# Sink rows of v: four small loads and one placement for the whole batch, instead of a selection matmul per sequence

## The chip, the cores and the metric

The kernel runs on one core of one Trainium2 chip. Of its engines five names occur here: PE (TensorE, matrix products; PEld is its weight load), DVE (VectorE), ACT (ScalarE), POOL (GpSimd) and SP (SyncE, which here only issues DMAs and waits). PE and DVE can work on PSUM, where matrix products land; PSUM has eight banks. The metric is the device time of one execution in microseconds (us), lower is better; it is the median of several runs. A profiled execution has a time of its own, and a span (first to last instruction) that is a little shorter than that time.

## The reference

Inputs: q, k, v of shape (batch 4, heads 8, positions 768, head size 64) in float32, two mixing vectors, and three weight matrices. First an attention in which every position sees the last 128 positions and, besides, the first four positions of its sequence (the sinks):

```python
is_sink = pos[None, :] < int(n_sink)          # n_sink = 4
rel = pos[:, None] - pos[None, :]
in_window = (rel >= 0) & (rel < int(window))  # window = 128
scores = np.where(is_sink | in_window, scale * q @ k.T, -1e9)
a = softmax(scores);  x = a @ v               # heads side by side: (4, 768, 512)
```

Its output x goes through a channel mix:

```python
xk = mu_k * x + (1 - mu_k) * x_prev           # x_prev: one position earlier
xr = mu_r * x + (1 - mu_r) * x_prev
k = np.maximum(xk @ w_k, 0)                   # 512 -> 1024  ("keys")
out = sigmoid(xr @ w_r) * (k * k @ w_v)       # "gates", and 1024 -> 512 ("product")
```

## The kernel before

**Units.** The work is cut into 12 units of 256 positions, three per sequence (`b` is the sequence, `T` the unit in it). A unit goes through `prepare` (its rows of q and k are cast to bf16 and transposed, its rows of v are cast into `vb`), `attend` (scores, exponentials `e` on ACT, a mask multiplied in by DVE, products with `vb`, division into `x`), `mix` (`x` transposed into `xt`, then `xk` and `xr` made by DVE) and `ffn` (the keys, `rl` and its square `kk`; the gates and `th`; the product and `ob`, which is stored). The `ffn` of a unit stands in the program beside the attention of the next one.

**The sinks.** The units with T = 1 and 2 also need the four sink positions of their sequence. Their scores come from `ksink`, a copy of four columns of the transposed keys; the exponentials are `es`. For the products with v there is one tile `vsink` of 128 partitions per sequence. Its partitions hold, in blocks of 32 for a pair of heads and of 4 rows for each of the two heads in it, the four sink rows of v for that head, next to a column of ones, and zeros for every other head. It is made like this: a product on PE (L814) with the 0/1 matrix `spread`, which copies rows 0 to 3 of the cast `vb` of the sequence's first unit, with all 512 columns of all heads, to every block; and a multiplication on DVE (L818) of the 512 columns in PSUM with the 0/1 tile `hmask`, which leaves to each partition its own head. This happens once per sequence, so four times, and there are two `vsink` tiles, whose column of ones is written once at the start by POOL (L642).

**PSUM.** Two tiles of two banks each hold scores; the other four banks form one pool ("bank"), from which every other product takes its place: transposes, sink scores, the product of L814, the products with v, keys, gates and products. A bank comes free when the engine that reads it is done.

**What sets the order.** Each operation is entered in a list with `P.op` and has a number. The tables `ORDER` (the sequence of numbers on each engine) and `CHOICE` (which of the engines allowed to an operation does it) are written out in the file; `schedule` (L195) follows them, and picks buffers and banks as it goes. On each engine the instructions run strictly in that sequence, and an instruction that waits holds up all behind it on its engine. Until about 28 us of planned time `schedule` also puts products without use into PE's gaps ("fill", on the tile `warm`).

**The start.** DVE clears tiles (L578 to L588). POOL makes the masks, `hmask`, the identity and `spread` (L594 to L642). ACT issues the two small loads of the mixing vectors, loads its table and runs one tiny exponential (L551, L560). SP issues all loads of q, k, v and the weights, first q and k of unit 0 in two halves each.

## Time and profile before

| what | value |
|---|---|
| median of 3 runs | 163.79 us (162.93 to 163.96) |
| the profiled execution: its time | 163.9 us |
| the profiled execution: its span | 162.2 us, granted PE clock 1.000 |
| busy in the span: PE, DVE, ACT, POOL | 152.7, 147.4, 119.9, 39.3 us |
| moved by DMA | 35.16 MB, mean 217 GB/s |

Busy time of PE counts products without use too, and the ends of products are modelled. The span is 1.7 us shorter than the execution's own time. In the views, a row of a timeline or of the chain begins with its start and its length in us; a row of a group gives busy time in us, the mean length of one instruction in ns, and the idle time of its engine just before the group's instructions, with what ended most of it; a row of waits gives the total in us, how often, and the longest.

### The profile page before, as it was taken

Reading aid. Unit: us, or ns where it says so; the run is one execution under the profiler, and the core shown is the slowest. Engines: PE = TensorE matmul, PEld = TensorE weight load, DVE = VectorE, ACT = ScalarE, POOL = GpSimd, SP = SyncE. Lnnn points to the kernel's source line nnn. Section 1 sums busy time; section 2 is a strip of 40 time slices with the busy share of each in tenths; the row PEclk is TensorE's granted clock in tenths of the full one; section 3 lists DMA queues with packets and bytes.
Section 4 is the critical chain, followed back from the end, with each engine's and each line's share of the span. In section 5 each row is a group of like instructions: output and inputs, shape, how many; then the busy total and the mean of one; then the engine's idle time right before and its main releaser. Section 6 shows DMA issues by size and latency. Waiting matters only on the chain.

```text
span 162.2 us, 4697 instructions
## 1 busy us (share of the span) xinstructions
PE 152.7 (94%) x1857; PEld 99.4 (61%) x1857; DVE 147.4 (91%) x378; ACT 119.9 (74%) x194; POOL 39.3 (24%) x69
## 2 busy tenths in 40 slices
PE   7959779999999999999999999999999999999992
PEld 2545457964568567776566575865466865577541
DVE  6299989999999999999999999999999999998631
ACT  4699998999999899888689964878167985043420
POOL 6643330610662260242111006241010040001000
PEclk9999999999999999999999999999999999999999
DMA  4999999999988999999999999999999733351113
GB/s 140 251 353 249 391 342 295 368 401 312 211 265 215 259 233 156 237 266 144 223 213 211 303 220 207 196 265 164 265 168 206 168 89 103 65 195 68 65 65 129
DMA packets 78885, 35.16 MB, mean 217 GB/s; under 512 B 68744, under 2 KB 71056, under 8 KB 78864
## 3 DMA queue, kind: packets, MB, share of 16 engines
q1 hardware_dynamic: 78384, 33.63, 88.7%
q0 software_dynamic: 320, 1.05, 1.8%
q8 instruction: 14, 0.23, 0.7%
q10 hardware_dynamic: 160, 0.20, 0.3%
q14 instruction: 7, 0.06, 0.1%
HBM read 24.12 MB, written 6.29 MB: 188 GB/s over the span
## 4 chain that ended last, share of the span: by engine, by line
PE 75%; DVE 7%; SPq 5%; DMA 5%; ACT 3%; issue 2%; POOL 1%; DVEq 0%
PE bank L1188 24%; PE bank L1139 22%; PE bank L1170 12%; PE bank L971 6%; DMA ks<-in_k_dram 5%; PE sc L866 5%; SPq L483 2%; DVE e L952 2%; SPq L500 2%; ACT rl L1149 2%; PE bank L1012 2%; PE bank L754 1%; PE bank L924 1%; SPq L507 1%; DVE x L988 1%
## 5 line engine op out<-in xcount | busy, mean ns | idle before, releaser
L1139 PE MATMUL bank<-xk,wk_sb 128*128 128x256 bf16 x384 | 48.3, 273 | 0.0
L938 ACT ACTIVATE e<-sc 128x1024 bf16<-128x1024 f32 (+1 forms) x48 | 45.0, 965 | 2.3 <-PE sc L866 2.1
L1188 PE MATMUL bank<-wv_h,kk 128*128 128x512 bf16 x184 | 44.8, 379 | 0.0
L1139 PEld LDWEIGHTS <-wk_sb 128*128 128x128 bf16 x384 | 36.0, 98 | 7.2
L1149 ACT ACTIVATE rl<-bank 128x512 bf16<-128x512 f32 x47 | 27.2, 608 | 15.6 <-PE bank L1139 13.8
L952 DVE TENSOR_TENSOR e<-e,mask 128x1024 bf16<-128x1024 bf16 (+1 forms) x48 | 31.0, 659 | 0.0
L1188 PEld LDWEIGHTS <-kk 128*128 128x128 bf16 x184 | 17.0, 98 | 15.8
L1061 DVE SCALAR_TENSOR_TENSOR xr<-td,mu_all,xt 128x256 bf16<-128x256 bf16 x48 | 24.0, 514 | 0.0
L1170 PE MATMUL bank<-wr_sb,xr 128*128 128x512 bf16 x96 | 23.7, 379 | 0.4 <-DVE vsink L818 0.4
L1061 DVE SCALAR_TENSOR_TENSOR xk<-td,mu_all,xt 128x256 bf16<-128x256 bf16 x48 | 23.9, 526 | 0.1
L1161 DVE TENSOR_TENSOR kk<-rl 128x512 bf16<-128x512 bf16 x48 | 20.9, 451 | 1.8 <-ACT rl L1149 1.7
L1176 ACT ACTIVATE th<-bank 128x512 f32<-128x512 f32 x24 | 14.1, 598 | 10.9 <-PE bank L1170 10.9
L988 DVE TENSOR_TENSOR x<-bank,rec 128x256 bf16<-128x256 f32 x48 | 19.4, 416 | 0.3
L1197 DVE SCALAR_TENSOR_TENSOR ob<-th,bank 128x512 f32<-128x512 f32 x23 | 15.5, 679 | 2.7 <-ACT th L1176 2.5
L971 PE MATMUL bank<-vb,e 128*128 128x65 bf16 x352 | 16.4, 194 | 1.3 <-DVE e L952 1.2
L791 POOL CAST vb<-vs 128x512 bf16<-128x512 f32 x10 | 9.4, 948 | 31.8 <-DMA vs<-in_v_dram 22.1
L971 PEld LDWEIGHTS <-e 128*128 128x128 bf16 x352 | 13.8, 97 | 5.4 <-DVE e L952 2.5
L1170 PEld LDWEIGHTS <-xr 128*128 128x128 bf16 x96 | 8.8, 98 | 9.3 <-issue 0.5
L866 PEld LDWEIGHTS <-kt 64*64 64x64 bf16 (+1 forms) x496 | 8.9, 106 | 6.4 <-issue 3.8
L866 PE MATMUL sc<-qt,kt 64*64 64x128 bf16 (+4 forms) x496 | 12.6, 226 | 0.0
L1048 DVE TENSOR_TENSOR td<-xt 128x512 bf16<-128x512 bf16 x24 | 10.6, 455 | 0.0
L714 POOL CAST qb<-qs 128x512 bf16<-128x512 f32 x7 | 5.1, 722 | 21.8 <-DMA qs<-in_q_dram 21.8
(95 smaller groups left out, 150.9 us busy)
## 6 DMA issues: line engine op xcount, KB each, us to landing
vs<-in_v_dram SPq DMA_DIRECT2D x24, 256.0 KB, 5.0
out_dram<-ob SPq DMA_DIRECT2D x19, 256.0 KB, 3.9
ks<-in_k_dram SPq DMA_DIRECT2D x16, 256.0 KB, 5.1
qs<-in_q_dram SPq DMA_DIRECT2D x12, 256.0 KB, 4.0
qs<-in_q_dram SPq DMA_DIRECT2D x6, 512.0 KB, 5.8
ks<-in_k_dram SPq DMA_DIRECT2D x4, 512.0 KB, 8.4
w<-in_moe_w_k_dram SPq DMA_DIRECT2D x2, 1024.0 KB, 8.8
w<-in_moe_w_v_dram SPq DMA_DIRECT2D x2, 1024.0 KB, 10.4
```

Of the source, the lines that this page charges most:

```text
L866: nc.tensor.matmul(out=sc[keys, a, o0 + f0 - q0:o0 + f1 - q0], lhsT=lhs[rows, keys], rhs=qs[rows, f0:f1], start=u not in BIAS, stop=True, ...
L938: nc.scalar.activation(out=buf[ek][:, :, lo:], in_=buf[sck][:, :, lo:], func=AF.Exp, scale=scale)
L952: nc.vector.tensor_tensor(out=at, in0=at, in1=m, op=ALU.mult)
L971: nc.tensor.matmul(out=o[:, g, a, :], lhsT=e[:, a, e0:e0 + 128], rhs=rhs, start=(T == 0 and i == 0), stop=(i == len(blocks) - 1), skip_gro ...
L988: P.op("DVE", dve(256), lambda ok=ok, rk=rk, c=c: nc.vector.tensor_tensor(out=buf["x", u][:, :, 128 * c:128 * c + 128].rearrange("p g (a d ...
L1061: nc.vector.scalar_tensor_tensor(out=buf[key][:, c, :], in0=buf[tk][:, i, :], scalar=mu[w][:, c:c + 1], in1=xt[:, c, t0 - 1:t0 + 255], op0 ...
L1139: nc.tensor.matmul(out=ps[:, i, :], lhsT=wk_sb[:, c, 128 * f:128 * f + 128], rhs=xk[:, c, :], start=(c == 0), stop=(c == NC - 1), skip_gro ...
L1149: nc.scalar.activation(out=buf[rk], in_=buf[psk].rearrange("p (i t) -> p i t", i=2), func=AF.Relu)
L1161: P.op("DVE", dve(512, 0.52), lambda f2=f2, rk=rk: nc.vector.tensor_tensor(out=buf["kk", u][:, 2 * f2:2 * f2 + 2, :], in0=buf[rk], in1=buf ...
L1170: nc.tensor.matmul(out=buf[psk], lhsT=buf["xr", u][:, c, 128 * g:128 * g + 128], rhs=wr_sb[:, c, :], start=(c == 0), stop=(c == NC - 1))
L1188: nc.tensor.matmul(out=buf[psk], rhs=wv_h[:, f, :], lhsT=buf["kk", u][:, f, 128 * g:128 * g + 128], start=(f == 0), stop=(f == NF - 1))
L1197: P.op("DVE", dve(512), lambda psk=psk, tk=tk, bk=bk: nc.vector.scalar_tensor_tensor(out=buf[bk], in0=buf[tk], scalar=1.0, in1=buf[psk], o ...
```

## The change

- `load_sinks`: ACT issues four DMAs, one for each sink position, each of 32 rows (sequence and head) of 64 numbers, into `vs32`, whose 128 partitions then hold every sink row of v.
- One cast of `vs32` to bf16 (`vs16`, on POOL), four products on PE of 64 columns each (one per sequence, with a `spread` that now has a 128x128 part for each sequence) into one bank, and one copy from there into `rows` (on ACT), a tile with 65 columns per sequence whose last column is one.
- `vsink` has four tiles, one per sequence; each is made by one DVE multiplication of 520 columns: the sequence's 65 columns of `rows`, repeated for the eight heads, times `hmask`. Both inputs are now in SBUF and in bf16.
- The products of L814 and the multiplications of L818 go, and with them the POOL copies of the column of ones (L642) and the clearing of `vsink`. `spread` is made by eight POOL copies in place of two; the clearing at the start has a larger `spread` and `rows` in it.
- `ORDER` and `CHOICE` are new tables. In sum over the kernel, DVE gets five `rl` from ACT, gives six casts of q to POOL and ACT, and POOL's four stores go to SP. One choice is narrowed: the weight cast of `wk` is no longer allowed on POOL.

```diff
@@ CHOICE, ORDER: new tables; the first rows of two of them
-        94, 91, 107, 78, 97, 100, 105, 118, 110, 115, 130, 136, 143, 133, 121, 139,
+        98, 81, 101, 112, 104, 107, 123, 115, 120, 77, 148, 135, 141, 131, 138, 144,
...
@@ tiles and clearing
-    spread = tile1([128, 128], BF16, "spread")
+    spread = tile1([128, B, 128], BF16, "spread")
+    vs32 = tile1([128, D], FP32, "vs32")
+    vs16 = tile1([128, D], BF16, "vs16")
+    rows = tile1([128, B, D + 1], BF16, "rows")
-    vsink = [tile1([128, H, D + 1], BF16, f"vsink{i}") for i in range(2)]
+    vsink = [tile1([128, H, D + 1], BF16, f"vsink{i}") for i in range(B)]
-        for t, value in ((ones, 1.0), (spread, 0.0), (hmask, 1.0)):
+        for t, value in ((ones, 1.0), (spread, 0.0), (hmask, 1.0), (rows, 1.0)):
-        for t in ksink + vsink:
+        for t in ksink:
@@ make_spread
-        for a in range(2):
-            nc.gpsimd.tensor_copy(
-                out=spread[0:NS, :].rearrange("p (c w) -> p c w", w=32)[:, :, 4 * a:4 * a + NS],
-                in_=ident[0:NS, 0:NS].unsqueeze(1).to_broadcast([NS, NP, NS]))
+        to = spread.rearrange("p b (k i w) -> p b i k w", k=2, i=2)
+        at = ident.rearrange("p (s b i k a) -> p a s b i k", s=NS, b=B, i=2, k=2)
+        for a in range(2):
+            for j in range(NS):
+                nc.gpsimd.tensor_copy(out=to[:, :, :, :, NS * a + j], in_=at[:, a, j])
@@ new
+    def load_sinks():
+        for j in range(NS):
+            nc.scalar.dma_start(out=vs32[B * H * j:B * H * j + B * H, :],
+                                in_=v[:, :, j, :].rearrange("b h d -> (b h) d"))
...
+    def spread_sinks():
+        for b in range(B):
+            nc.tensor.matmul(out=buf["vsp"][:, D * b:D * b + D], lhsT=spread[:, b, :], rhs=vs16,
+                             start=True, stop=True)
...
+    for b in range(B):
+        P.op("DVE", dve(520, 0.52), lambda b=b: nc.vector.tensor_tensor(
+            out=vsink[b], in0=rows[:, b, :].unsqueeze(1).to_broadcast([128, H, D + 1]),
+            in1=hmask, op=ALU.mult), 30 * b - 30, port=True, reads=["rows", "hmask"],
+            writes=[("vsink", b)])
@@ prepare, for the first unit of a sequence
-        P.op("PE", 220.0, lambda: nc.tensor.matmul(
-            out=buf[psk].rearrange("p (h d) -> p h d", h=H), lhsT=spread,
-            rhs=buf["vb", u][:, 0, :, 0:D], start=True, stop=True), rank + 4,
-            take=[("bank", psk)], hold=[("vb", u)], reads=["spread", ("vb", u, 0)], writes=[psk])
-        P.op("DVE", dve(512), lambda: nc.vector.tensor_tensor(
-            out=vsink[b % 2][:, :, 0:D], op=ALU.mult, in1=hmask[:, :, 0:D],
-            in0=buf[psk].rearrange("p (h d) -> p h d", h=H)), rank + 4, hold=[psk],
-            reads=[psk, "hmask", "sinks"], writes=[("vsink", b % 2)])
```

How the new tables move instructions is shown at three places. A row names the line, the operation, and the tile written, an arrow, the tiles read. First ACT at the very start. Before:

```order
L551 DMA ob_134<-in_moe_mu_r_dram 4x128
L560 ACT_TABLE_LOAD
L560 ACTIVATE tiny<-warm 128x2
L551 DMA ob_134<-in_moe_mu_k_dram 4x128
L719 CAST qb_82<-qs_70 128x4x2x64
L777 COPY qt_89<-bank_63 128x512
L777 COPY kt_85<-bank_66 128x512
L938 ACTIVATE e_93<-sc_61 128x2x384
```

And now (`vs_150` is `vs32`, L665 is `load_sinks`):

```order
L552 DMA ob_134<-in_moe_mu_r_dram 4x128
L561 ACT_TABLE_LOAD
L561 ACTIVATE tiny<-warm 128x2
L665 DMA vs_150<-in_v_dram 32x64 x4
L746 CAST kb_79<-ks_67 128x4x2x64
L746 CAST qb_82<-qs_70 128x4x2x64
L804 COPY qt_89<-bank_64 128x512
L552 DMA ob_134<-in_moe_mu_k_dram 4x128
L681 CAST rows<-bank_66 128x4x64
L954 ACTIVATE e_93<-sc_61 128x2x384
```

The four loads stand ahead of the first casts, both first casts are ACT's (DVE had one of them), and the copy into `rows` stands ahead of the first exponential. On PE the four products of `spread_sinks` stand between the first transposes of k and those of q of unit 0, ahead of the first scores.

Second, POOL at the start, before:

```order
L594 AFFINE_SELECT mask<-ones 128x128 x2
L594 AFFINE_SELECT hmask<-hmask 128x4x65 x4
L594 AFFINE_SELECT ident<-ones 128x128
L594 AFFINE_SELECT ident<-ident 128x128
L603 CAST ident_143<-ident 8x8
L594 AFFINE_SELECT mask_147<-ones 128x128 x3
L613 MEMSET mask_147 4x256
L642 COPY vsink_153<-hmask 128x8
L642 COPY vsink_154<-hmask 128x8
L630 COPY spread<-ident 4x4x4 x2
L719 CAST kb_79<-ks_67 128x4x2x64
```

And now (`vs_151` is `vs16`, `mask_147` is the mask of the first unit):

```order
L598 AFFINE_SELECT ident<-ones 128x128
L598 AFFINE_SELECT ident<-ident 128x128
L607 CAST ident_143<-ident 8x8
L598 AFFINE_SELECT hmask<-hmask 128x4x65 x4
L598 AFFINE_SELECT mask<-ones 128x128 x2
L636 COPY spread<-ident 128x4x2x2 x8
L669 CAST vs_151<-vs_150 128x64
L598 AFFINE_SELECT mask_147<-ones 128x128 x3
L617 MEMSET mask_147 4x256
L746 CAST kb_79<-ks_67 128x4x2x64
L746 CAST qb_82<-qs_70 128x4x2x64
```

`spread` and the cast of the sink rows, which waits for the four loads, now stand ahead of the first unit's mask and of the second halves' casts.

Third, DVE at the first unit of the last sequence, before:

```order
L952 TENSOR_TENSOR e_97<-e_97,mask_147 128x2x384
L952 TENSOR_TENSOR e_95<-e_95,mask_147 128x2x384
L818 TENSOR_TENSOR vsink_154<-bank_65,hmask 128x8x64
L952 TENSOR_TENSOR e_93<-e_93,mask_147 128x2x384
L952 TENSOR_TENSOR e_96<-e_96,mask_147 128x2x384
L1197 SCALAR_TENSOR_TENSOR ob_134<-th_128,bank_63 128x512
```

And now:

```order
L968 TENSOR_TENSOR e_97<-e_97,mask_147 128x2x384
L968 TENSOR_TENSOR e_95<-e_95,mask_147 128x2x384
L1177 TENSOR_TENSOR kk_121<-rl_126 128x512
L1213 SCALAR_TENSOR_TENSOR ob_134<-th_131,bank_65 128x512
L1001 RECIPROCAL rec_101<-bank_63 128x4
L968 TENSOR_TENSOR e_93<-e_93,mask_147 128x2x384
L688 TENSOR_TENSOR vsink_159<-rows,hmask 128x520
L1004 TENSOR_TENSOR x_107<-bank_63,rec_101 128x2x128
```

The multiplication no longer reads a bank of PSUM.

107 lines of the change are left out of this document (59 added, 48 removed), and 139 rows, old and new, of the table ORDER.

## Prediction

> **What bounds the kernel now.** First the page: busy time of the engine with the most of it, and the slices of PE and DVE in tenths, each slice 4 us long.
>
> ```profile
> PE 152.7 (94%) x1857; PEld 99.4 (61%) x1857; DVE 147.4 (91%) x378; ACT 119.9 (74%) x194; POOL 39.3 (24%) x69
> ...
> PE   7959779999999999999999999999999999999992
> ...
> DVE  6299989999999999999999999999999999998631
> ```
>
> PE has gaps only in the first six slices, DVE is full almost as long and runs out before PE does. The table by stretches says where PE begins to be full, and what is full before that (columns: length, then busy time of PE, PEld, DVE, ACT, POOL):
>
> ```profile
> 15.00:20.00 5.00, 3.62 (x68) 1.98 (x66) 4.91 (x13) 4.98 (x8) 1.65 (x3) 1.00 0.99 361
> 20.00:25.00 5.00, 3.78 (x75) 2.63 (x72) 4.35 (x11) 4.34 (x7) 1.63 (x2) 1.00 1.12 339
> 25.00:30.00 5.00, 4.95 (x76) 4.16 (x76) 5.00 (x13) 4.58 (x8) 0.64 (x1) 1.00 1.05 324
> 30.00:35.00 5.00, 4.71 (x74) 3.99 (x74) 5.00 (x12) 5.00 (x9) 2.88 (x3) 1.00 1.03 380
> 35.00:40.00 5.00, 5.00 (x69) 2.63 (x59) 4.97 (x16) 4.91 (x8) 0.00 (x0) 1.00 1.11 351
> ```
>
> Up to 35 us ACT and DVE are the full ones, and PE waits for what they hand over. From 35 us on PE is full. The chain that ended last, in order of time, agrees:
>
> ```profile
> 10.17 8.74 DMA ks<-in_k_dram
> 18.97 0.82 POOL kb L710
> ...
> 20.70 0.42 DVE xt L1021
> ...
> 35.88 1.73 PE bank L1170 x8
> ...
> 108.22 1.80 DVE e L952 x2
> 110.02 0.61 DVE vsink L818
> 110.67 1.02 PE bank L1170 x4
> ```
>
> It runs over a load and DVE, then over PE from the first gate products (L1170) at 35.88 to the end, but for one place, at 108 to 111 us. So I split the time at the first gate product. From there on both orders hold the same PE products, except that three of the four selection products (L814) are gone; I counted them row by row, 1435 before and 1432 now. What the change is worth is then: how much later or earlier the first gate product comes, less three products, less the stall at 110 us.
>
> **What goes from the full stretch.** Eight products of 512 columns take 1.73 us in the chain, 0.216 each. Three go: -0.65 us. The stall is in the list of waits, and the groups name its two sides:
>
> ```profile
> PE bank L1170 <- DVE vsink L818: 0.4, 1, 0.4
> ```
>
> ```profile
> L818 DVE TENSOR_TENSOR vsink<-bank,hmask 128x512 bf16<-128x512 f32 x4 | 2.7, 681 | 0.0
> ...
> L1153 DVE TENSOR_SCALAR rl<-bank 128x512 bf16<-128x512 f32 x1 | 0.7, 687 | 0.0
> ...
> L1161 DVE TENSOR_TENSOR kk<-rl 128x512 bf16<-128x512 bf16 x48 | 20.9, 451 | 1.8 <-ACT rl L1149 1.7
> ```
>
> The gate product needs a bank that L818 was still to read, and L818 stood behind two masks. Now the multiplication reads `rows` in SBUF, holds no bank, and at this place stands behind work that PE does not wait for. I take -0.4 (the wait in the list); at worst another reader of a bank is late there and nothing is won, 0. The new multiplication has no row here. Its nearest is the 512-column square of L1161, bf16 from SBUF, 0.451; the upper end is the old 0.681. I take 0.46, as types and size are those of L1161: 4 x 0.22 = 0.9 us less for DVE. Five `rl` at 0.687 come to DVE and six casts of q go, so over the whole kernel its load stays about even, and I give that nothing.
>
> **What is added at the start.** Four loads on ACT, eight copies of `spread` and a cast on POOL, four products on PE, one copy on ACT; all in front of the first scores. The rows, from the timeline:
>
> ```profile
> 1.47 0.26 ACTq L551 DMA_DIRECT2D ob<-in_moe_mu_k_dram  x1
> ...
> 2.69 0.20 ACT L560 ACTIVATE tiny<-warm 128x2 bf16<-128x2 bf16 x1
> ...
> 3.76 0.62 ACT L719 CAST qb<-qs 128x512 bf16<-128x512 f32 x1 [0.87 <-DMA qs<-in_q_dram]
> ...
> 4.56 0.97 POOL L594 TENSOR_SCALAR_AFFINE_SELECT mask<-ones 128x128 bf16<-128x128 bf16 x3
> ...
> 5.37 0.59 ACT L777 COPY qt<-bank 128x512 bf16<-128x512 bf16 x1 [0.99 <-PE bank L759]
> ...
> 6.63 0.51 PE L866 MATMUL sc<-qt,kt 64*128 64x256 bf16 x8
> ...
> 7.01 1.51 ACT L938 ACTIVATE e<-sc 128x768 bf16<-128x768 f32 x2 [0.43 <-PE sc L866]
> ...
> 7.63 0.40 PE L759 MATMUL bank<-ident,qb 128*128 128x128 bf16 x4
> ```
>
> And from the groups and the DMA view (last number: us from issue to landing):
>
> ```profile
> L842 ACT ACTIVATE es<-bank 128x256 bf16<-128x256 f32 x8 | 3.2, 402 | 2.6 <-PE bank L835 2.6
> ...
> L630 POOL COPY spread<-ident 4x16 bf16<-4x16 bf16 x2 | 0.3, 186 | 0.0
> ```
>
> ```profile
> out_dram<-ob POOLq DMA_DIRECT2D x4, 256.0 KB, 3.8
> out_dram<-ob ACTq DMA_DIRECT2D x1, 192.0 KB, 1.9
> ```
>
> ACT is free at 2.89. An issue on its queue takes 0.26 in the row above; with 32 descriptors in place of 4 I take 0.38, so the fourth load is issued at 4.0 and ACT is free for its first cast at 4.4 instead of 3.76. Landing: between 1.9 us (the store of ACT's queue, with the DMAs idle at the end) and 3.8 (POOL's, amid other traffic), so 5.9 to 7.8; I take 6.3, since it is 8 KB and not 256. POOL has done the same masks as before at 4.56, then needs 8 x 0.186 = 1.5 for `spread`, to 6.05, so the load comes last; its cast is another 0.2: 6.5. On PE the four small products (no row; they have an eighth of the 0.216 us columns each, and I take 0.06 apiece) stand ahead of the transposes of q: 6.5 + 0.25 + 0.40, then the copy 0.59 and two handovers of some 0.05: scores at 7.8 instead of 6.63, +1.2. ACT has the copy into `rows` in front of the first exponential, 0.40 as for the 256 columns of L842: +1.6.
>
> From the first exponential to the cast of `wr_sb`, which the first gate product needs, ACT has by the orders the same exponentials and weight casts, two casts and one copy more (0.62 and 0.59), and three `rl` fewer at about 0.6: 1.83 - 1.8 = 0. So it stays 1.6 late, less what it waited for others before:
>
> ```profile
> 20.26 0.59 ACT L772 COPY kt<-bank 128x512 bf16<-128x512 bf16 x1 [0.28 <-PE bank L754]
> ...
> 21.25 0.38 ACT L842 ACTIVATE es<-bank 128x256 bf16<-128x256 f32 x1 [0.40 <-PE bank L835]
> ```
>
> These waits, 0.28 and 0.40, hang on the load of k that lands at 18.97, not on ACT's own start, so 0.7 of the lateness is absorbed there: +0.9 at the first gate product. Bounds: at least 0 (sink rows cast at 6.1 as POOL allows, 1.2 late, and the later waits taken in too); at most the landing at 7.8, which is 1.5 later than taken, and nothing absorbed: +3.1. DVE is no longer the last in this stretch: it hands seven fp32 casts on and gets two `rl`, one PSUM copy and one weight cast there, nominally 1.8 us less to do.
>
> The sum on the profiled execution: 163.9 + 0.9 - 0.65 - 0.4 = 163.75. The median of the runs, 163.8, is 0.1 lower, which makes **163.6 us**. POOL's four stores on SP cost nothing, since SP only waits, for 17.5 us in its store line alone by the waits of its queue:
>
> ```profile
> SPq L1204 <- DVE ob L1197: 17.5, 7, 7.7
> ```
>
> **A rule that speaks against the change.** Two masks of 768 columns take 1.80 us in the chain at 108.22, and 1.2 by the mean of their group; a POOL cast runs beside them:
>
> ```profile
> L952 DVE TENSOR_TENSOR e<-e,mask 128x768 bf16<-128x768 bf16 x16 | 9.3, 600 | 0.0
> ```
>
> ```profile
> 108.50 0.62 POOL L714 CAST qb<-qs 128x512 bf16<-128x512 f32 x1
> ```
>
> So a DVE operation on two SBUF tiles can lose 0.6 us to one POOL cast. The Trainium skill, "GPSIMD Engine Reference", section "Key points", says that POOL shares its SBUF interfaces with DVE and contends with DVE instructions that have two SBUF inputs. That agrees with these rows, and by it the sum would be that of the second rival.
>
> **The rivals.** *Faster: DVE and not ACT sets the first gate product.* For: DVE is 5.00 of 5.00 from 25 to 35, the chain runs over it from 20.70, and it gets 1.8 us less to do, of which a start 0.9 later leaves 0.9. Against: the same rows show ACT at 4.58 and 5.00. Then the gate comes 0.9 earlier: 163.8 - 0.9 - 0.65 - 0.4 = 161.85.
>
> *A little slower: contention of POOL and DVE.* The multiplication had one input in PSUM and now has both in SBUF, and POOL gets three casts more over the kernel. Three multiplications and three casts at 0.6 make 3.6 us; against that stands DVE's idle time (third busy number) in the two stretches before the end, 0.75 + 1.41 = 2.2, where it runs out before PE does:
>
> ```profile
> 145.00:150.00 5.00, 5.00 (x40) 3.72 (x38) 4.25 (x11) 2.17 (x4) 0.54 (x1) 1.00 0.28 109
> 150.00:155.00 5.00, 5.00 (x30) 2.74 (x28) 3.59 (x8) 1.68 (x3) 0.00 (x0) 1.00 0.14 52
> ```
>
> That leaves +1.4: 165.0.
>
> *Slower: the sink rows come late.* They stand in PE's queue ahead of the first scores, so every stage of unit 0 waits for four loads of 8 KB. With a landing at 7.8 it is the +3.1 from above: 163.8 + 3.1 - 0.65 - 0.4 = 165.85. It decides once the lateness at the first gate product passes 2.7 us. For: the loads of q and k are in flight at that time. Against: a separate queue and a tiny amount.
>
> That the change does nothing it says is ruled out by the orders: the three products are gone.
>
> **How the numbers follow.** The forecast gets 0.45, faster 0.22, contention 0.12, late sink rows 0.21. A measurement of this kernel tells about 1% (1.6 us: 162.2 and 165.4) from no change. Faster by more than that: the first rival, and a little of the forecast's lower end, 0.23. Slower: the last rival, and a little of contention, 0.23. The rest, 0.54, is within 1%. The range reaches from 161.6, just under the faster case, to 165.7, just under the slower one's price; about 0.1 is left out on each side.
>
> **What would show it.** Right: L676's products at about 6.5 and the first scores at about 7.8 in the timeline; the first gate product near 36.8; PE full from there; no wait of PE for a multiplication of `vsink`; that multiplication at about 460 ns. Wrong: a first gate product before 35.5 (DVE was the bound) or after 38 (late sink rows); masks or multiplications of more than 1 us beside POOL casts and PE gaps behind them; or new PE gaps after 40 us, which the sum leaves out altogether because the new order's waits in that stretch are not in this trace.

## The result, and the profile after

The changed kernel takes 168.67 us (median of 4 runs, 167.93 to 169.75); the kernel before takes 163.49 in the same comparison (162.93 to 163.96). The ratio is 1.032, with a 95% interval of 1.025 to 1.039: slower, and outside the range that was given. The profiled execution took 168.96 us, its span is 167.0, the granted clock 0.999. Against the profiled execution before (163.9, span 162.2) that is 5.1 us: 4.85 in the span and 0.2 around it. In the experiments below a median is over all executions, while a ratio leaves out executions over 1.5% longer than the shortest of their kernel, so the two can differ.

The page of the changed kernel, busy time and the slices of PE and DVE (about 4.2 us each):

```profile
PE 155.9 (93%) x1860; PEld 100.5 (60%) x1860; DVE 147.1 (88%) x376; ACT 119.8 (72%) x194; POOL 38.0 (23%) x72
...
PE   7389799989999999999999999999999999999992
...
DVE  5108999999999999999989999999999899999841
```

The second and third digits are new: DVE stands still from about 4 to 12 us (1 and 0), and PE has a 3. Table by stretches, first the kernel before, then the changed one (columns: length, then busy time of PE, PEld, DVE, ACT, POOL, the granted clock, the DMA share):

```profile
5.00:10.00 5.00, 3.99 (x39) 2.22 (x37) 2.48 (x7) 4.07 (x7) 2.49 (x9) 1.00 1.09 277
```

```profile
0.00:5.00 5.00, 3.88 (x6) 1.31 (x7) 2.14 (x15) 2.29 (x4) 3.66 (x18) 1.00 0.57 159
5.00:10.00 5.00, 1.31 (x13) 1.14 (x13) 0.69 (x1) 0.35 (x1) 1.75 (x10) 1.00 1.03 243
10.00:15.00 5.00, 5.00 (x33) 2.39 (x33) 2.31 (x5) 3.48 (x6) 2.67 (x6) 1.00 1.14 333
```

From 5 to 10 us DVE does 0.69 us of work and ACT 0.35. The chain of the changed kernel up to the first scores (L882) says why (start, length, what):

```profile
0.80 3.01 DMA ks<-in_k_dram
3.82 0.02 issue
3.84 4.99 DMA vs<-in_v_dram
8.83 0.06 issue
8.88 0.25 POOL vs L669
9.13 0.04 issue
9.17 0.37 PE bank L676 x4
9.54 0.43 PE bank L786 x4
9.97 0.96 PE bank L1270 x2
10.93 0.43 PE bank L1267
```

The fourth sink load is issued at 3.84, just after the first half of k has landed, and lands 4.99 us later. That it waits for a load with which it has nothing to do is in the program. The program numbers its DMAs over eight semaphores that the queues of SP and ACT share, so a DMA waits before its issue until the one eight places earlier has landed; for the fourth sink load that is the first half of k. In the timeline the first three leave one behind the other, and the fourth only when that half has landed:

```profile
0.80 0.46 SPq L508 DMA_DIRECT2D ks<-in_k_dram  x1
...
1.44 1.26 ACTq L665 DMA_DIRECT2D vs<-in_v_dram  x3
...
3.84 0.32 ACTq L665 DMA_DIRECT2D vs<-in_v_dram  x1
```

The waits of POOL and of PE between 4 and 12 us, one line each, are this landing and what hangs on it:

```profile
POOL vs L669 <- DMA vs<-in_v_dram: 3.2, 1, 3.2
```

```profile
PE bank L676 <- POOL vs L669: 3.7, 1, 3.7
```

On PE the transposes of q stand behind the four products. On POOL, behind the cast, stand a mask of the first unit and the casts of the second halves of its k and q (timeline of POOL):

```profile
8.88 0.24 POOL L669 CAST vs<-vs 128x64 bf16<-128x64 f32 x1 [3.25 <-DMA vs<-in_v_dram]
9.07 0.81 POOL L598 TENSOR_SCALAR_AFFINE_SELECT mask<-ones 128x128 bf16<-128x128 bf16 x3
9.83 0.30 POOL L617 MEMSET mask<- 4x256 bf16 x1
10.08 0.60 POOL L746 CAST kb<-ks 128x512 bf16<-128x512 f32 x1
10.63 0.60 POOL L746 CAST qb<-qs 128x512 bf16<-128x512 f32 x1
```

Before, the cast of k's second half began at 6.27. The first scores come at 11.29 (before 6.63), the first gate product (now L1186) at 40.1 (before 35.7). From there to the last product it is 123.3 us, before 122.8. So 4.4 us of the loss were there by the first gate product, 0.5 came later, 0.2 lies outside the span.

### The profile page after: what moved, and what is told of

Same layout as the page of the kernel before. It is cut to its first block, busy times and chain, and to the rows that moved or that the text cites. A ratio compares the mean times of both kernels' runs of the same rounds, so it can differ in the third digit from the quotient of the medians.

```text
span 167.0 us, 4729 instructions
## 1 busy us (share of the span) xinstructions
PE 155.9 (93%) x1860; PEld 100.5 (60%) x1860; DVE 147.1 (88%) x376; ACT 119.8 (72%) x194; POOL 38.0 (23%) x72
## 4 chain that ended last, share of the span: by engine, by line
PE 64%; DVE 19%; DMA 8%; ACT 5%; issue 2%; DVEq 0%; POOL 0%
PE bank L1155 19%; PE bank L1204 18%; PE bank L1186 10%; PE bank L987 5%; PE sc L882 4%; DVE e L968 4%; DMA kt<-kb 3%; DMA vs<-in_v_dram 3%; ACT e L954 3%; DVE xk L1077 3%; DVE kk L1177 2%; DVE ob L1213 2%; DMA ks<-in_k_dram 2%; PE bank L1270 2%; DVE xr L1077 1%
## 5 line engine op out<-in xcount | busy, mean ns | idle before, releaser
L1165 ACT ACTIVATE rl<-bank 128x512 bf16<-128x512 f32 x42 | 24.6, 608 | 14.4 <-PE bank L1155 13.2
L968 DVE TENSOR_TENSOR e<-e,mask 128x1024 bf16<-128x1024 bf16 (+1 forms) x48 | 32.1, 681 | 0.2 <-ACT e L954 0.2
L1186 PE MATMUL bank<-wr_sb,xr 128*128 128x512 bf16 x96 | 23.5, 379 | 0.3 <-DVE ob L1213 0.3
L1077 DVE SCALAR_TENSOR_TENSOR xr<-td,mu_all,xt 128x256 bf16<-128x256 bf16 x48 | 22.8, 488 | 0.0
L1177 DVE TENSOR_TENSOR kk<-rl 128x512 bf16<-128x512 bf16 x48 | 20.4, 442 | 0.4 <-ACT rl L1165 0.4
L818 POOL CAST vb<-vs 128x512 bf16<-128x512 f32 x13 | 10.8, 832 | 36.4 <-DMA vs<-in_v_dram 27.8
L1186 PEld LDWEIGHTS <-xr 128*128 128x128 bf16 x96 | 9.0, 98 | 9.8 <-issue 0.5
L882 PE MATMUL sc<-qt,kt 64*64 64x128 bf16 (+3 forms) x496 | 12.9, 227 | 0.4 <-DMA kt<-kb 0.3
L882 PEld LDWEIGHTS <-kt 64*64 64x64 bf16 (+1 forms) x496 | 9.1, 107 | 5.4 <-issue 3.6
L741 POOL CAST kb<-ks 128x512 bf16<-128x512 f32 x5 | 3.4, 671 | 31.7 <-DMA ks<-in_k_dram 31.7
```

Source lines behind the costliest of these rows:

```text
L882: nc.tensor.matmul(out=sc[keys, a, o0 + f0 - q0:o0 + f1 - q0], lhsT=lhs[rows, keys], rhs=qs[rows, f0:f1], start=u not in BIAS, stop=True, ...
L968: nc.vector.tensor_tensor(out=at, in0=at, in1=m, op=ALU.mult)
L1077: nc.vector.scalar_tensor_tensor(out=buf[key][:, c, :], in0=buf[tk][:, i, :], scalar=mu[w][:, c:c + 1], in1=xt[:, c, t0 - 1:t0 + 255], op0 ...
L1165: nc.scalar.activation(out=buf[rk], in_=buf[psk].rearrange("p (i t) -> p i t", i=2), func=AF.Relu)
L1177: P.op("DVE", dve(512, 0.52), lambda f2=f2, rk=rk: nc.vector.tensor_tensor(out=buf["kk", u][:, 2 * f2:2 * f2 + 2, :], in0=buf[rk], in1=buf ...
L1186: nc.tensor.matmul(out=buf[psk], lhsT=buf["xr", u][:, c, 128 * g:128 * g + 128], rhs=wr_sb[:, c, :], start=(c == 0), stop=(c == NC - 1))
```

## The experiments

Theory L: all that matters is that POOL and PE wait, each at one place of its fixed order, for a late last sink row. The rivals are that the new orders are worse in themselves (O), and that ACT's queue and the displaced loads of SP are late (Q, S). Four kernels were to tell them apart.

**e1: the loads without the wait.** The four loads go to a tile that nobody reads; the cast reads zeros, so the sinks' rows of v are left out of the result.

```diff
-            nc.scalar.dma_start(out=vs32[B * H * j:B * H * j + B * H, :],
+            nc.scalar.dma_start(out=unread[B * H * j:B * H * j + B * H, :],
```

> The changed kernel with its four small DMAs kept on ACT's queue, but written to a tile that nobody reads; the tile that POOL casts is filled with zeros by DVE at the start. This leaves out the sinks' rows of v (the four products place zeros), and keeps all orders and all transfers. Theory L (the late fourth sink row holds up POOL's cast, PE's products behind it and all that PE and POOL have in their order after them): the wait goes, the first scores come back from 11.29 us to 6.6 to 7.3, the first gate product from 40.09 to 35.7 to 36.5, and the time from 168.67 to about 164.3 us (163.9 to 165.0; what stays over 163.5 is the stretch after the first gate product, +0.4, and up to 0.5 of the ACT queue, which still waits for the fourth issue until 3.84). Rival O (the newly found orders are worse in themselves, and the start would have been made up later): 167 us or more. Rival Q (ACT's queue and SP's loads, held by the fourth DMA's issue at 3.84 and by the displaced loads, are what is late): first scores still after 9 us, time 166.5 or more.

Measured: median 164.98 us against 164.21, ratio 0.995 (0.989 to 1.000). First scores at 7.5, first gate product at 36.2. The same loads on the same queues at the same times, in the same orders, delay the first gate product by 0.5 us when nobody waits for them, and not by 4.4: as the cause of the late start O, Q and S fall. For the rest of the kernel O does not fall. Four of the ten executions took 162.4 to 163.9 us, the other six 164.9 to 166.5, all with a granted clock of 0.997 or more. The profiled one is the longest, and from its first gate product to the last product it takes 124.6 us, 1.8 more than before. So the new orders may cost up to that much behind the start; no run here holds this apart.

**e2: one DMA instead of four.** The rows then land in another order, and the 0/1 table `spread` is permuted to match (not shown).

```diff
-        for j in range(NS):
-            nc.scalar.dma_start(out=vs32[B * H * j:B * H * j + B * H, :],
-                                in_=v[:, :, j, :].rearrange("b h d -> (b h) d"))
+        nc.scalar.dma_start(out=vs32, in_=v[:, :, 0:NS, :].rearrange("b h j d -> (b h) j d"))
```

> The changed kernel with one DMA of 128 rows in place of the four of 32 (the tile's partitions are then in the order sequence, head, position, and the table that places them is permuted to match); everything else and all orders as in the changed kernel. Theory L: with one DMA there is no ninth DMA that waits for an earlier one before its issue; issued at 1.4 to 1.5 us and landed 2.6 to 3.6 us later, as the first two of the four, the rows are there by 5.1 us, POOL's cast follows the table's end at 5.6, the scores come at 7.0 to 7.8 us, the first gate product at 36.0 to 36.9, the time is 164.2 to 165.2 us. Rival (small rows land late whenever they are issued, since SP's loads fill the DMA queues from 2 us on): landing 6.5 or later, and the time 166 or more. Rival O (orders): 167 or more.

Measured: median 165.29 us against 164.21, ratio 1.000 (0.995 to 1.005). The timeline:

```profile
1.49 0.65 ACTq L664 DMA_DIRECT2D vs<-in_v_dram  x1
...
5.93 0.24 POOL L667 CAST vs<-vs 128x64 bf16<-128x64 f32 x1 [0.18 <-DMA vs<-in_v_dram]
...
7.39 0.51 PE L880 MATMUL sc<-qt,kt 64*128 64x256 bf16 x8
```

Issued at 1.49 and landed 4.4 us later, later than the 5.1 expected, but POOL waits only 0.18 for it; scores at 7.39, first gate product at 36.1. As L has it. Here too the executions spread: six took 163.6 to 165.6 us, four 166.3 to 167.9.

**e3: the steps behind.** Four DMAs as they are; the consumers move back in the orders. In the trace ACT's and DVE's steps stand one place earlier than the expectation says, behind the third exponential and the third reciprocal:

```
POOL  before: spread x8, [cast of sinks], mask x3, memset, second halves of k and q
      now:    spread x8, mask x3, memset, second halves of k and q, [cast of sinks]
PE    the four products: behind the first two value products of the first unit
ACT   the copy into rows: behind the first unit's third exponential
DVE   the first multiplication: behind the first unit's third reciprocal
```

> The changed kernel with its four DMAs as they are, but with four steps moved back in the orders: POOL's cast of the sinks' rows behind its casts of the second halves of the first unit's k and q, PE's four products behind the first two value products of the first unit, ACT's copy of the rows behind the first unit's four exponentials, DVE's first multiplication behind the fourth reciprocal. Theory L: the landing at 8.8 us meets a cast at 9 to 10 and nobody waits for it; scores at 6.7 to 7.5 us, first gate product at 35.7 to 36.9, time 164.0 to 165.2 us. Rival Q (the late issue of the fourth DMA on ACT's queue and the displaced loads of SP are what costs, not the wait behind the landing): scores after 9 us, time 166.5 or more. Rival O: 167 or more.

Measured: median 165.95 us against 164.21, ratio 1.010 (1.006 to 1.013), so 0.8 us more than expected at its upper end, but by the ratios 2.2% under the changed kernel. The rows still come at 8.8, scores at 6.67, first gate product at 36.7. The landing did not change; what stood behind it did.

**e9: POOL's cast left in front.** As e3, but POOL's order is that of the changed kernel.

> The third experiment once more (four DMAs; PE's products, ACT's copy and DVE's first multiplication moved behind the first unit's start), but with POOL's cast of the sinks' rows left where the changed kernel has it, ahead of the last mask and of the casts of the second halves of the first unit's k and q. It tells which engine's queue passes the wait on. If it was PE's queue (the products stood ahead of the transposes of q): as the third experiment, first gate product at 36.4 to 37.0, time 165 to 166. If POOL's queue counts as well: first scores early (6.6 to 7 us), but the second halves cast at 10.1 and 10.6 us as in the changed kernel, so the second pair of scores at 12 to 13.5 us, the first gate product at 37.5 to 39, time 166.3 to 168.

Measured: median 169.56 us against 164.18, ratio 1.033 (1.027 to 1.038), just the changed kernel's. First gate product at 39.8. Timeline of PE and POOL:

```profile
6.66 0.51 PE L877 MATMUL sc<-qt,kt 64*128 64x256 bf16 x8
...
8.87 0.24 POOL L664 CAST vs<-vs 128x64 bf16<-128x64 f32 x1 [3.22 <-DMA vs<-in_v_dram]
...
10.07 0.60 POOL L741 CAST kb<-ks 128x512 bf16<-128x512 f32 x1
10.62 0.60 POOL L741 CAST qb<-qs 128x512 bf16<-128x512 f32 x1
...
10.73 0.40 PE L781 MATMUL bank<-ident,kb 128*128 128x128 bf16 x4 [3.56 <-POOL kb L741]
```

PE no longer waits for the sinks and does its first scores at 6.66, as before the change. But it waits 3.56 us for the cast of k's second half, which POOL has behind the sinks' cast. So POOL's queue alone is enough for nearly the whole delay, more than was expected of it: the first gate product comes 4.1 us later than before the change, in the changed kernel 4.4. What PE's queue would do alone is not tested. In the changed kernel two engines waited in parallel for one landing; e3, which moves POOL's cast as well, has its first gate product 3.1 us earlier than e9.

**e6: the four loads first on ACT's queue.** Nothing is eight places ahead of them; the fourth leaves at 2.2 us.

```
ACT   before: load of mu_r, table load, tiny exponential, four sink loads, casts
      now:    four sink loads, load of mu_r, table load, tiny exponential, casts
```

> The changed kernel with its four sink DMAs at the head of ACT's queue, ahead of the load of mu_r and of the table load, so that none of them comes behind eight other DMAs; the fourth then leaves at about 2.0 us instead of 3.84. All else as in the changed kernel. Theory W (what is late is the fourth DMA's issue, held until an earlier load had landed): landing 2.6 to 3.6 us after issue, so all rows by 4.6 to 5.6 us, POOL's cast at 5.6, first scores at 7 to 8 us, first gate product at 36 to 37, time 164 to 165.3. Rival T (a small DMA among SP's loads lands 5 us after its issue or later, whenever it is issued): rows at 7 us, scores at 8.9 or later, time 165.8 or more. Rival S (the displaced loads of SP take the wait over: the first unit's second half of q or its v comes late): scores early, but first gate product at 38 or later.

The profiled execution took 163.91 us, and its view of the loads is

```profile
L660 ACTq DMA_DIRECT2D vs<-in_v_dram x4: 436/440/448, 0.8 to 2.2; - x4
...
DMA to landing us min/median/max: 2.1/3.1/3.9
```

so the last row landed by 6.1; scores at 8.24, first gate product at 36.7. That is what theory W expects of the start, 0.2 us late in the scores. But the other three executions took 166.55, 167.70 and 168.53, at a granted clock of 1.00 like the first. The median of all four is 167.13 against 164.58; the ratio of 1.020 (1.012 to 1.027) rests on the three long ones. No trace of those is there. The early issue is shown to help in one execution; whether the rows, or the loads of SP that now stand behind them, come late in the others stays open.

**e8: one DMA, issued later.** Orders of the kernel before (as e4, below), the load behind the first two exponentials, the consumers just ahead of their use.

```
ACT   before (e4): tiny exponential, [sink load], mu_k, cast of q, copies, two exponentials
      now:         tiny exponential, mu_k, cast of q, copies, two exponentials, [sink load]
POOL  the cast behind ksink; PE, ACT and DVE 1 to 3 us later than in e4
```

> As the fourth experiment (one DMA, the new way of placing, orders and engines of the kernel before), but the sinks' load leaves ACT's queue behind the first unit's first two exponentials, at about 8.5 us, and the cast, products, copy and first multiplication come 1 to 3 us later still, just ahead of the first use at about 18 us. If the load among the early loads was what cost the fourth experiment its start (first gate product at 36.2 against 35.7): first gate product at 35.5 to 35.9 and a time 0.3 to 0.6 us under the fourth's, a ratio to before of 0.996 to 1.001. If its loss lies in the dense stretch: ratio 1.003 to 1.007, as the fourth. If the steps of the prediction on the dense stretch hold once the start is undisturbed: ratio 0.993 to 0.995.

Measured: median 166.59 us against 164.58, ratio 1.014 (1.009 to 1.020): slower than e4, and none of the three outcomes expected. The load, issued at 7.82, lands 5.7 us later, and POOL waits again, now with another cast behind it:

```profile
11.40 0.44 POOL L827 COPY ksink<-kt 64x16 bf16<-64x16 bf16 x2
13.67 0.48 POOL L661 CAST vs<-vs 128x64 bf16<-128x64 f32 x1 [1.82 <-DMA vs<-in_v_dram]
14.10 0.61 POOL L729 CAST qb<-qs 128x512 bf16<-128x512 f32 x1
```

The first gate product comes at 38.2. It looks like the same fault at another place, and I had made it again: POOL's queue got a wait on a small load amid large ones. How much of the 2.5 us at the first gate product is due to it stays open, since in this execution the granted clock was 0.90 from 20 to 25 us and 0.76 from 25 to 30, too. The other five executions, with a clock of 0.997 or more, took 165.7 to 167.9.

**e5: without the products on zeros.** In the changed kernel 9.97 to 11.36 of the chain are products without use, planned for gaps that the late start had closed.

```diff
             if isinstance(i, tuple):
-                self.fill(*i[1:])
+                fills += 1
+                if fills not in range(3, 9):
+                    self.fill(*i[1:])
```

> The changed kernel, sinks' DMAs and waits as they are, without the products on zeros (lines 1267 and 1270 of the changed kernel's profile) that the planner puts into PE's order from behind the first transposes to the first unit's second half; those before 4.9 us stay. Nothing of the computation is left out. Theory F (they were planned for PE's free time; behind a PE that runs 3.7 us late, 1.4 us of them stand in the way of the first scores and 2 us more of them behind): first scores at 10.0 to 10.6 us in place of 11.29, first gate product 1 to 2 us before 40.1, time 166.7 to 167.9. Rival (the scores wait for ACT's copy of q's transposes, POOL's casts and the loads anyway): first gate product at 39.6 or later, time 168.3 or more. A third way: PE's granted clock falls for want of work, and the time rises above 169.

Measured: median 168.76 us against 164.58, ratio 1.024 (1.015 to 1.032). First scores at 10.72 instead of 11.29, 1.38 us after the four products began instead of 2.12; first gate product at 40.0, as in the changed kernel. The table by stretches shows a fall of the granted clock (the number before the last two):

```profile
10.00:15.00 5.00, 3.54 (x38) 2.62 (x37) 2.87 (x7) 4.21 (x8) 3.40 (x8) 0.50 1.12 336
15.00:20.00 5.00, 4.61 (x37) 3.16 (x37) 4.55 (x12) 4.37 (x8) 3.70 (x6) 0.53 0.99 319
```

It was 0.50 for 10 us. In the changed kernel, with nearly the same wait of 3.7 us ahead, the column says 1.00, but there too the products themselves were slow for some time. Four transposes, first in the changed kernel, then in e5:

```profile
9.36 0.61 PE L786 MATMUL bank<-ident,qb 128*128 128x128 bf16 x4
...
16.49 0.40 PE L1028 MATMUL bank<-ident,x 128*128 128x128 bf16 x4
```

```profile
9.45 0.60 PE L789 MATMUL bank<-ident,qb 128*128 128x128 bf16 x4
...
20.47 0.40 PE L784 MATMUL bank<-ident,qb 128*128 128x128 bf16 x4
```

A product without use of 512 columns takes 0.63 us at 12.45 and 0.38 at 14.18 in the changed kernel; in e5 it is still 0.61 at 19.25. So in these two executions the products without use cost 0.7 us at the scores, and with them PE is at its full speed some 6 us sooner. That the clock is why nothing was won is not shown. One of the four executions of e5 had a granted clock of 0.997 and took 169.49. And e9 gives another reason, close to the rival of the expectation: with scores at 6.66 its first gate product still comes at 39.8, since POOL's casts are as late. Either way, leaving these products out is no repair.

**e4: the new placement in the old orders.** One DMA, and `ORDER` and `CHOICE` of the kernel before; the new steps come behind the first unit's start, and nobody waits for the load.

```
POOL  spread behind the first cast of k, the sinks' cast behind the first cast of v
PE    the four products behind the transposes of the first x
ACT   the load behind the tiny exponential, the copy behind the fourth exponential
DVE   the multiplications where they were, the first a few steps later
```

> The new way of placing the sinks' rows (one DMA, four products, one copy, multiplications out of SBUF) in the orders and the engine choices of the kernel before; the new steps are put behind the first unit's start: cast on POOL behind the first cast of v, products on PE behind the second exponential's value products, the copy on ACT behind the first unit's fourth exponential, multiplications where DVE had them (the first one a few steps later). By the steps of the prediction that are about the rest (three wide products less, -0.65; the stall at 110.67 gone, -0.4; shorter multiplications) this should take 162.4 us (162.0 to 162.9) and be the fastest of all. Rival D (the dense stretch gives nothing back, as in the changed kernel, where the part from the first gate product to the last came out 0.4 us longer and not 1.05 shorter, since other waits follow): 163.2 to 163.9 us. Rival H (the sink rows' DMA among the early loads costs the start 1 us or more wherever it is read): 164.3 or more.

Measured: median 165.02 us against 164.21, ratio 1.0055 (1.0015 to 1.0095). No wait for the sinks is left, and still it is 0.9 us slower than the kernel before, not 1.1 faster. First gate product at 36.2; from there 123.8 us, before 122.8. So the second step of the prediction was wrong too, and three rivals of it remain: PE's products save nothing, DVE's shorter work saves nothing, the added steps cost it.

**e7, e12, e13: what went, taken out of the kernel before.** Orders unchanged; for sequences 1 to 3 the wide product (e12), the multiplication (e13) or both (e7) are left out, and with them the right sink values of these sequences.

```diff
-        P.op("PE", 220.0, lambda: nc.tensor.matmul(
+        P.op("PE", 220.0, lambda: b or nc.tensor.matmul(
...
-        P.op("DVE", dve(512), lambda: nc.vector.tensor_tensor(
+        P.op("DVE", dve(512), lambda: b or nc.vector.tensor_tensor(
```

> The kernel before, orders unchanged, without the wide placing product and the multiplication out of the bank for sequences 1, 2 and 3 (the sinks' values of these sequences are left out or those of an earlier one). This takes away all that the change was to save in the dense stretch, and adds nothing. By the prediction's terms (three products of 0.216 us on a full PE, and a stall of 0.4 us): 162.4 to 163.1 in a set of runs where before takes 163.5, a ratio of 0.9936 (0.991 to 0.997). Rival D (the dense stretch is held by DVE, loads and small waits by turns, so that PE's saved time turns into another wait): ratio 0.998 to 1.002. Rival V (DVE is the bound there, and three multiplications of 0.68 less give it 2 us): ratio 0.990 or less.

> The kernel before, without the three wide placing products of sequences 1 to 3; the multiplications stay and read whatever the bank holds (the sinks' values of these sequences are left out). If PE is the bound of the dense stretch, as the prediction had it, three products of 0.216 us: -0.65, a ratio of 0.996 (0.994 to 0.998), and the next experiment gives 0.997 to 1.000. If DVE's time is what counts: 0.999 to 1.001 here, and the gain in the next.

> The kernel before, without the three multiplications of sequences 1 to 3 (the sinks' values of these sequences are left out or those of an earlier one); the products stay. It takes 3 x 0.681 us from DVE and the stall of 0.4 us from PE. If PE is the bound: -0.4 at most, ratio 0.997 to 1.000. If DVE is: the whole of the seventh experiment's gain, ratio 0.993 to 0.996.

Measured: both out, 163.77 us against 164.58, ratio 0.995 (0.992 to 0.999), -0.8 us. Products alone out: 164.13 against 164.38, 0.998 (0.994 to 1.002). Multiplications alone out: 164.27 against 164.38, 0.999 (0.995 to 1.002). All of it together is worth 0.8 us, and either part alone less than can be told from nothing. The 1.05 us of the prediction lie within the interval of e7, but e7 also gives DVE 2.0 us of multiplications, of which the change gives back only a part.

**e14: e4 without what was added.** No load, no `spread`, no cast, no four products, no copy; the multiplications out of SBUF stay, and work on ones.

> The fourth experiment (new placement in the orders of the kernel before) without what the placement adds at the start: no DMA of the sinks' rows, no placing table on POOL, no cast, no four products, no copy on ACT; the four multiplications out of SBUF stay and work on ones (the sinks' values are left out). If the added steps cost the start and nothing else is wrong with the prediction's steps: first gate product back at 35.7, and the ratio to before 0.993 to 0.996, that is 1.5 us under the fourth. If the added steps are hidden and the dense stretch gives nothing back: 1.000 to 1.004, close to the fourth's 1.0055.

Measured: 164.45 us against 164.38, ratio 1.0035 (1.0003 to 1.0067). So of e4's 0.9 us some 0.3 may be the added steps, which is within the scatter; by the ratio the rest is there without them, by the medians nothing of it is. The first gate product is not back at 35.7: in the profiled execution (166.09 us, with a granted clock of 0.84 from 20 to 25 us and 0.82 from 25 to 30) it comes at 36.3. The old orders with the new multiplications give nothing back that I can measure.

**e10, e11: attempts at the best of both.** e10 is e2 with the single DMA at the head of ACT's queue. e11 is e3 with the single DMA of e2, and `spread` moved behind the second halves on POOL as well.

```
e10  ACT   [one sink load], load of mu_r, table load, tiny exponential, casts
e11  POOL  mask x3, memset, second halves of k and q, spread x8, [cast of sinks], ksink
```

> One DMA for the sinks' rows, and it leaves at the head of ACT's queue at 0.8 us, ahead of the load of mu_r and of the table load; orders of the changed kernel otherwise. In the runs so far the time from issue to landing was 2.1 to 3.9 us for issues at 0.8 to 2.2, 3.6 to 4.4 at 1.5, 5.0 at 3.84 and 5.8 at 7.8. So rows by 4 to 4.8 us, POOL not waiting (its table ends at 5.6), scores at 7.0 to 7.8, first gate product at 36.0 to 36.5: a ratio to before of 0.994 to 1.001, as the first two experiments, and fewer long executions than the sixth, whose last rows were the last thing POOL waited for. If the long executions come from elsewhere (the stretch after the first gate product), they stay, and the ratio is 1.003 or more.

> One DMA at 1.5 us, and on all four engines the sinks' steps behind the first unit's start (PE's products, ACT's copy and DVE's multiplication as in the third experiment; on POOL the placing table and the cast behind the casts of the second halves of k and q). Nothing of the sinks then stands ahead of the first scores: scores at 6.6 to 7.0 us, second halves cast 1 us sooner than in the second experiment, first gate product at 35.5 to 36.2. With the saving of the seventh experiment (0.8 us) a ratio to before of 0.993 to 0.999. If the added work itself costs the start (ACT's copy of 0.38 us, DVE's ones of 0.28, POOL's table of 1.2 us, in a stretch in which DVE and ACT are busy all the time): first gate product at 36.2 to 36.8, ratio 0.999 to 1.005.

Measured: e10 166.19 us, ratio 1.013 (1.007 to 1.019); e11 166.27 us, ratio 1.013 (1.008 to 1.018), against 164.18. Nobody waits for the rows in either (landed 3.2 and 3.5 us after issue). Scores at 7.60 and 6.84, first gate products at 37.1 and 36.5; from there to the last product 123.0 and 123.2. They miss what I expected by 1 to 2%, and no complete version made here beats the kernel before.

## Why the prediction was wrong

On the profiled executions the sum was 5.2 us short (163.75, measured 168.96): 3.5 us at the first gate product (+0.9 forecast, +4.4 measured), 1.5 in the full stretch behind it (-1.05 forecast, +0.5 measured), and 0.2 outside the span.

**The landing of the fourth sink load: the step that failed.** It was taken at 6.3, bounded at 7.8, and is 8.83, which is 2.5 of the 3.5 us. The table on POOL was ready at 5.63, not 6.05, so the load came last by more than 3 us. The issue was placed well, 4.0 against 3.84, for a wrong reason: not ACT's own work but the landing of an earlier load set it. From issue to landing I took 2.3 us and bounded it by 3.8, the landing of large stores late in the program; measured 4.99. The rival "the sink rows come late" had the mechanism, at 0.21 and +2.0 us; its point against, "a separate queue and a tiny amount", was no reason. The Trainium skill, "DMA: Bandwidth & Descriptors", section "Issuing engines are not separate DMA queues", says that DMAs started by different engines run on the same 16 DMA engines and interleave. The loads here fit that: 2.6 us for the quickest of the four, 4.99 for the last. While it was under way (3.84 to 8.83 us) 3226 packets of SP's queue were moved and 127 of ACT's, and from 5 to 10 us the DMA share was 1.03.

**What waits behind it.** I followed PE's queue (products, transposes, scores) and ACT's. POOL's I left out, though the cast stands there in front of a mask and two casts that the first unit needs. e9 shows that this queue alone is enough for the delay (first gate product at 39.8).

**From the landing to the first gate product** the working came out in the one traced execution in which the landing is the one assumed. In e6's profiled execution the rows landed at 6.1, the scores came at 8.24 (7.8 forecast), the first gate product at 36.7 (36.8), and the time was 163.91 (163.75). The three other executions of e6 took 166.6 to 168.5, so this is one case and no proof. With the landing at 8.83 two more terms fail: the products without use add 0.7 us behind the late PE, and of the delay of 4.8 at the first exponential (11.83, before 7.01) 4.4 arrive at the first gate product. So 0.4 or 0.5 are absorbed, not 0.7.

**DVE and not ACT as bound of the start** (the faster rival, 0.22): not decided by these runs in its own terms. What the late start lost shows on both: from 0 to 36 us DVE is busy 25.8 us and ACT 25.9, before 30.6 and 30.9.

**The full stretch: the second step that failed.** I forecast -1.05 us, three products and the stall; measured +0.5. The stall is gone as forecast (nobody waits for L688), but "PE full from there" does not hold. The whole stretch in the table, before and then now:

```profile
35.70:158.50 122.80, 122.43 (x1437) 78.95 (x1434) 116.37 (x292) 89.39 (x147) 24.59 (x35) 1.00 0.91 193
```

```profile
40.10:163.40 123.30, 122.10 (x1433) 78.62 (x1430) 116.44 (x295) 89.81 (x147) 20.10 (x27) 1.00 0.83 183
```

PE has 0.3 us less to do, but stands idle for 1.2 us in place of 0.4; DVE's work is the same. The list of PE's waits, which before has the stall alone, now has four others in this stretch, three of them for a DVE instruction that reads a bank:

```profile
PE bank L1186 <- DVE ob L1213: 0.3, 1, 0.3
PE bank L1155 <- DVE ob L1213: 0.3, 1, 0.3
PE sc L882 <- DMA kt<-kb: 0.3, 1, 0.3
PE bank L781 <- DVE ob L1213: 0.2, 1, 0.2
```

These are the "new PE gaps after 40 us" that the prediction names as a sign of being wrong. The error is that PE was taken as the only bound; in the first 19 us of that stretch DVE is as full as PE:

```profile
35.70:54.40 18.70, 18.70 (x210) 11.43 (x207) 18.67 (x48) 18.45 (x30) 5.79 (x9) 1.00 1.00 262
```

```profile
40.10:59.30 19.20, 18.96 (x213) 11.43 (x210) 19.17 (x49) 17.89 (x30) 5.84 (x7) 1.00 0.77 181
```

The first line is before, the second the changed kernel, nearly the same piece of the work: DVE full in both, 0.5 us longer, and PE no longer full. The sizes were fair as a sum (e7: -0.8), but the new placement does not give them back reliably: in the profiled executions with the new orders the stretch takes from 121.9 us (e6) to 124.6 (e1), where 121.75 was forecast. Why stays open in part: e14 against e7 leaves 1.3 us (ratios 1.0035 and 0.9953) that no row names, and the single executions scatter by as much.

**The multiplication and contention.** Estimated 0.46 us, bounds 0.451 to 0.681; measured 0.42 twice and 0.83 twice. DVE's multiplications at 44.57 and 117.67, and POOL's casts nearest to them:

```profile
44.57 0.83 DVE L688 TENSOR_TENSOR vsink<-rows,hmask 128x520 bf16<-128x520 bf16 x1
...
117.67 0.42 DVE L688 TENSOR_TENSOR vsink<-rows,hmask 128x520 bf16<-128x520 bf16 x1
```

```profile
44.32 0.80 POOL L818 CAST vb<-vs 128x512 bf16<-128x512 f32 x1
...
117.86 0.70 POOL L741 CAST qb<-qs 128x512 bf16<-128x512 f32 x1 [1.99 <-DMA qs<-in_q_dram]
```

The two that start inside a POOL cast (at 14.57 and 44.57) take twice the time of the two that start ahead of one (at 80.54 and 117.67). The contention rival (0.12) thus had a true mechanism, worth 2 x 0.41 = 0.8 us of DVE's time on the multiplications, for which it assumed 1.8. The other half of its 3.6 us, three more POOL casts, is not told apart by these runs.

## What to carry to other kernels

Where a change puts a wait into an engine's queue, write down for each engine that waits, directly or through another, what stands behind it; here POOL's queue alone was enough for the loss at the start, and following only the engines that used the data missed it. Price a small load by small loads issued at that time amid that traffic, and look which earlier DMA its issue waits for. Before you count a saving on one engine, look whether another is as full in the same stretch, as DVE was here, and take the work out of the old kernel alone to see what it is worth.

## What the runs showed of the hardware

Of the landing of a small load (8 KB, or 32 KB in one DMA): the later it was issued, the longer it took. Of 8 KB: issued at 0.8 us 2.1 (e6), at 1.44 us 2.6 and at 3.84 us 5.0 (the changed kernel). Of 32 KB: at 0.8 us 3.2 (e10), at 1.5 us 3.5, 3.6 and 4.4 (e11, e4, e2), at 7.8 us 5.7 (e8). In the changed kernel the DMA share was 0.57 in the first 5 us and 1.03 and 1.14 in the next two stretches of 5 us; whether the time of the issue or the traffic then is what counts, these runs do not hold apart.

Of DVE and POOL: a cast of POOL that starts inside a multiplication gets longer as well. The third multiplication of the changed kernel keeps its 0.42 us, and the cast, 0.60 at 10.08 us when DVE stands still, takes 1.09:

```profile
80.54 0.42 DVE L688 TENSOR_TENSOR vsink<-rows,hmask 128x520 bf16<-128x520 bf16 x1
```

```profile
80.67 1.09 POOL L741 CAST qb<-qs 128x512 bf16<-128x512 f32 x1 [3.94 <-DMA qs<-in_q_dram]
```

The Trainium skill, "SBUF — State Buffer", section "SBUF: two separate sides", calls the ports that the two share an exclusive lock, which whoever starts first keeps for the whole instruction. The multiplications fit that: 0.42 us when they start first, 0.83 when the cast does. The casts fit it in direction only: this one is 0.49 us longer, though the multiplication ends 0.29 us after the cast's start, and DVE's next instruction on SBUF tiles (`kk`, at 80.88) may have its part; the one at 117.86 takes 0.70.

Of the clock: a wait of PE of 3.8 us, ahead of which four transposes took 0.61 us, and behind it a PE that was busy 71% of the next full 5 us, went with a granted clock of 0.50 and 0.53 in two stretches (e5). A wait of 3.7 us, also behind transposes of 0.61, followed by a PE busy 5.00 of 5.00, left the column at 1.00, but the transposes still took 0.61 at 9.36 and 12.04 (the changed kernel). A wait of 3.56 us, ahead of which they had already come down to 0.39, was followed by transposes of 0.40 at once (e9). So the granted clock of 1.00 in a stretch at the start does not by itself say that PE ran at full speed there; the lengths of equal products do. Each is one execution.
